# A fused spectral-mixing and gated-FFN kernel: the transfers of two small matrix sums move from the second run to the first, and some low parts, sums and silus change places

## The chip, the core and the metric

The kernel runs on one core of a Trainium2 chip. The metric is device time in microseconds (us), the median of several executions. The engines that appear below are PE (matrix multiply; its weight loads are listed as PEld), DVE (vector), ACT (activation), POOL and SP. SP and POOL also issue transfers (DMAs); each of them issues its own in program order.

## The reference

A layer norm of x (2048 tokens, 448 features) feeds two branches, whose product is added to x:

```python
xn = _layernorm(x, axis=-1)
a = jnp.einsum("bsd,ed->bse", xn, dft_hid_re)
b = jnp.einsum("bsd,ed->bse", xn, dft_hid_im)
s = jnp.einsum("ts,bse->bte", dft_seq_re, a) - jnp.einsum("ts,bse->bte", dft_seq_im, b)
g = _silu((_gelu(xn @ w_gate) * (xn @ w_up)) @ w_down)
return x + s * g
```

Everything is float32, the FFN has 1792 hidden columns, and x comes twice as the same array.

## The kernel before

Every float32 operand of a matmul is used as two parts: a high part, which ACT copies out in a rounded type, and a low part, which DVE makes as the value minus the high part. A product of two such operands takes three matmuls (high by high, high by low, low by high). The instruction order on each engine is written out by hand; nothing reorders it later.

**Stage 1, the FFN (up to about 403 us).** The 2048 tokens are four quarters of 512. Hidden columns come in blocks of 128, `f` = 0 to 13. After a start on the first two blocks, two runs follow: `p` = 0 (quarters 0 and 1) and `p` = 1 (quarters 2 and 3), each over `f` = 2 to 13, 24 blocks in all. A block is one call of `strassen`, which forms gate and up for both quarters with Strassen-like products `x1` to `x6`, and runs between them the down projections of an earlier pair of blocks (`down_one`, L439: tiles `po`, which DVE adds to `gacc` in L452). Between the products of a block three steps `prep` make the weights of the next block: ACT's plain high parts (L352), POOL's sums of weight parts (`sums_s`, L337 to L343), ACT's high parts of these sums (L356, L357), DVE's low parts (L353, L360, L361) and then SP's load of the weights after that (`load_s`, L319 and L320, into `raw`). `sums_s` also pops the list `adds`, behind its first sum: transfers that POOL issues with accumulation, among them those that form the sums of the sequence matrices in `sums` (L959). ACT's gelu of the first product is L526. In the first run and at the start of the second, `t_step` makes the operand sums of the second run: a DVE subtraction (L875), ACT's high part (L880) and DVE's low part (L884), from tiles that `t_load` brings into `tmp` (L860, L864).

Two buffers in DRAM, `e1[0]` and `e1[1]`, hold sums of the hidden-dimension DFT matrix `et`: `e_first` loads them (L1056, SP) and adds a second part with three POOL transfers (L1057, L1060). It is called in block `f` = 2 of the second run, and `e1` is read in the blocks `f` = 4 and 9 of that run. DVE's further sums of `et` (`e_sum`, L1064) end in `eq`, which SP stores in block `f` = 11 (`eq_store`, L1107).

**Stage 2, the hidden-dimension DFT (about 403 to 482 us).** Its order is the table `HID`: words such as `4.mm` (the matmuls of token tile 4), `4.ev` (ACT copies them out, L1386 and L1387), `4.sm` (four DVE sums, L1376 to L1379), `4.ca` and `4.lo` (high and low part, L1398 and L1401), `P3.le` (the low part of tile 15, L1345), `q.l` (three low parts of `eq`, L1087 and L1091), `s.3` and `s.all` (the last eight `po` tiles), `c.l4`, `c.s2`, `c.h2`, `c.d2` (load, sums, high part and low part of unit 4 or 2 of stage 3). A `c.d` issues a load into the place that it has read (`c.d0` unit 3, `c.d1` unit 6, `c.d2` unit 7).

**Stage 3, the sequence DFT (from about 482 us).** Eight pairs of row tiles `j`, each with 14 units `u` of Strassen-like products (L1534 high, L1537 low), then two plain tiles `t0`, `t1` (L1560). Per unit, `load_c` brings the matrices (L1439, L1440), `sum_c` adds (L1446, L1447), `high_c` and `low_c` split (L1454, L1458). The last pair gathers the products (`gather`, L1567 to L1575), takes silu of the FFN result (`gx`, loaded by L1514; L1639, L1693), multiplies and adds x, and stores.

Places that several of these share: unit 4 and 5 of stage 3 are loaded into the tile `f1`, which also holds tile 6 of stage 2 until `6.lo` has read it. In the lists of order below the names carry the program's own buffer numbers.

Of the kernel before, what the change touches and what calls it, by code (L numbers as in the profile page):

```python
# [10 lines left out]
AF = mybir.ActivationFunctionType  # L11
# [35 lines left out]
NS = len(KS)  # L47

LAST = 3


HID = """
0.mm l.0 q.h l.1 s.3 q.l 0.ev 0.sm 0.ca s.all 0.lo g.st 1.mm 1.ev 1.sm
P0.x1 P0.m 1.ca P0.x2 P0.u P0.x3 P0.c21 P0.x4 P0.be 1.lo P0.x1b P0.ac P0.x6 P0.bc P0.sc P0.cc
P0.x4b P0.ae P0.se 2.mm P0.ce P0.lc 2.ev P0.le 2.sm
P1.x1 P1.m 2.ca P1.x2 P1.u P1.x3 P1.c21 P1.x4 P1.be 2.lo P1.x1b P1.ac P1.x6 P1.bc P1.sc P1.cc
# [2 lines left out]
P2.x4b P2.ae  # L59
P3.x1 P3.m P2.ce P2.cc P3.x2 P3.u P3.x3 P3.c21 P2.le P3.x4 P3.be P3.x6 t.0 P2.lc P3.bc  # L60
P3.x1b P3.ac P3.sc P3.cc P3.x4b P3.ae c.l0
4.mm P3.ce P3.lc P3.le c.l1 c.l2 t.1 4.ev 4.sm 4.ca c.s0 c.s1
5.mm 4.lo 5.ev c.h0 5.sm c.d0 5.ca c.s2 6.mm 5.lo 6.ev 6.sm
7.mm c.h1 c.d1 c.h2 c.d2 6.ca c.s3 6.lo c.l4 c.l5 7.ev
"""


# [8 lines left out]
def fnet_geglu(ctx: ExitStack, tc: tile.TileContext, xw, ca, ct, cp, et, wss, wd, out):  # L76
# [495 lines left out]
    with tc.manual_schedule():  # L572
# [479 lines left out]
        e1 = [dram.tile([P, D], F32, name=f"e1{i}") for i in range(2)]  # L1052

        def e_first():
            for i in range(2):
                nc.sync.dma_start(e1[i], et[3 * i, :, 1])  # L1056
            adds.append(lambda: nc.gpsimd.dma_start(e1[0], et[1, :, 1], accum_op=ALU.add))  # L1057
            for r in (slice(0, 64), slice(64, P)):
                adds.append(
                    lambda r=r: nc.gpsimd.dma_start(e1[1][r], et[2, :64, 1], accum_op=ALU.add)  # L1060
                )

        def e_sum(to, a, b, n=P):
            return lambda: nc.vector.tensor_sub(*[e_part(i)[:n] for i in (to, a, b)])  # L1064
# [28 lines left out]
        def e_steps(f):  # L1093

            return {
                5: [e_sum(6, 0, 1), e_sum(5, 4, 0)],
                6: [e_sum(7, 2, 5), nop, es_high],
                7: [nop, es_low(0)],
                9: [nop, es_low(1), e_next],
                11: [e_sum(6, 2, 3), e_sum(7, 5, 2, n=64), then(e_sum(8, 0, 7), eq_store)],  # L1100
            }.get(f, [])

        def eq_at(i):
# [24 lines left out]
        for n, (p, f) in enumerate(blocks):  # L1128
            g = f // 2
            dn, q = [settle, send2] * 2, tq[p]  # L1130
            if n == len(blocks) - 2:
                v = sb.tile([P, 4096], FR, name="w2", tag="u0")
                slots.append((v[:, :WH], v[:, WH : WH + WL]))
                w2[0] = v
            prep = weights(n + 1)
            step = [e_steps(f)] if p else []
            if f % 2 == 0 and n:
                d_raw[0] = load_d(GROUPS[g])
            sum_step(n)
            if f % 2 and 1 < n < len(blocks) - 1 or n == len(blocks) - 2:  # L1140
                prep[1].append(lambda: weights_d(g))
                prep[2].append(lambda: low_of[g]())
            if p == 0:
                if f == 2:
                    dn = [nop, send, nop, send]
                    nc.sync.dma_start(gsp[0], gacc[2].rearrange("p k d -> p (k d)"))
                elif f == 3:
                    dn = [nop, send, send, low_d]
                if 6 <= f < 12:
                    step = [t1_steps[f - 6]]  # L1150
                elif f == 12:
                    step = [t1_steps[6][:1]]
                if f in (8, 11):

                    k = slice(0, 4, 3) if f == 8 else slice(1, 3)
                    for i in range(2):
                        v, w = [u[:, i * 2048 :][:, :2048] for u in (sp, a_x[1].bitcast(F32))]
                        v, w = [u.rearrange("p (k d) -> p k d", k=4)[:, k] for u in (v, w)]
                        nc.sync.dma_start(v, w)
            elif f == 2:  # L1160
                q = None
                for v, w in zip(prep, t1_steps[6][1:]):
                    v.append(w)
                dn[3] = then(send2, *t1_steps[7][:2])
                e_first()
            elif f == 3:

                late = then(late[0], t1_steps[7][2]), late[1]
                v = sb.tile([P, 8 * D], F32, name="gacc2", tag="u1")
                for c in range(2):  # L1170
                    gacc[2 + c] = part(v, c * 4 * D, 4, D)
                    nc.sync.dma_start(v[:, c * 4 * D :][:, : 4 * D], gsp[c])
            elif f == 4:
                e_begin()
            elif f == 5:
                nc.sync.dma_start(gs[:, : 8 * D], a_g[0])
            elif f == NF - 3:
                e_load(2)
            elif f == NF - 2:
                dn[2] = send2  # L1180
                prep[2].append(lambda: e_split(2))
                prep[2].extend([lambda b=b: e_load(b) for b in (1, 0, 3)])
            elif f == NF - 1:
                prep[1].append(lambda: e_split(0))
                prep[2].extend([lambda: e_split(3), lambda: e_split(1)])
                dn = [settle, send2, settle, nop]
                eq_load()
            while adds and n == len(blocks) - 1:
                adds.pop(0)()
            if step:  # L1190
                for v, w in zip(prep, step[0]):
                    v.append(w)
            prep = [then(*v) for v in prep]
            late = strassen(f, p, w_of[p, f], q, late, dn, prep)
            if p == 0 and f == 4:
                nc.sync.dma_start(gsp[1], gacc[3].rearrange("p k d -> p (k d)"))
            elif p == 0 and f == 5:
                t_load(0, 1, 0, 1)
            elif p == 0 and f == 9:
                t_load(0, 1, 3, 2)  # L1200
            if f % 2:
                dq += [(g, c, w_d[g], kk) for c in (2 * p, 2 * p + 1) for kk in range(4)]
# [313 lines left out]

        LOAD_AT = 2
        STORE_AT = 6, 9
        GX_AT, GX_END = (NS, 0), NS - LAST - 4

        PARTS = slice(0, 6, 5), slice(2, 4), slice(4, 7, 2), slice(1, 2)
        PRODUCTS = {1: (1, 0), 6: (3, 5), 2: (2, 2), 7: (5, 3), 5: (4, 4), 3: (6, 6), 4: (0, 1)}
# [73 lines left out]
        for m, (j, k) in enumerate(units):  # L1596
# [37 lines left out]
            if end and u == NS - LAST:  # L1634
# [1 line left out]
                prep_c(m + 4)  # L1636

                c12_6, c11_2, c21_7, c12_5, c22_5, c12_3, c21_4 = gather(ps)
                nc.scalar.activation(g_[0], gx[0], AF.Silu)  # L1639
                gather_1 = lambda: nc.vector.tensor_add(c1, c1, cs[1][1])  # L1640
                for f in (c12_6, c21_7, c12_5, c22_5, c21_4, gather_1, c11_2):
                    f()
# [5 lines left out]
            elif end and u > NS - LAST:  # L1648
                if u == NS:
                    py0 = py  # L1650
                if m < len(units) - 1:
                    continue
                y = raw_at(m + 3)[:, :D]
                nc.vector.tensor_add(c0, c0, py0[:, :D])
                nc.vector.tensor_mul(c0, c0, g_[0])
                nc.vector.tensor_add(c0, c0, x_[0])
                nc.sync.dma_start(ov[:, NK - 2], c0)
                halves_ = [
                    (e, eng, lambda p=p, e=e: nc.vector.tensor_mul(y[:, e], g_[1][:, e], p[:, e]))
                    for p, e, eng in zip(both_, sides, (nc.scalar, nc.sync))  # L1660
                ]
                for e, eng, times_ in halves_:
                    times_()
                    nc.vector.tensor_add(c1[:, e], c1[:, e], y[:, e])
                    eng.dma_start(ov[:, NK - 1, e], c1[:, e])
            elif u == NS - 1 and not end:
                todo = gather(ps)
                for f in todo[:3]:
                    f()
                prep_c(m + 3)  # L1670
            elif u == NS and not end:
                for f in todo[3:]:
                    f()
                prep_c(m + 3)
                nc.scalar.activation(kept, py[:, :D], AF.Copy)
            elif u == NS + 1:
                prep_c(m + 3)
                spare = [lambda: nc.vector.tensor_add(c0, c0, kept)]
                spare += give(j, 0)
                spare.append(lambda py=py: nc.vector.tensor_add(c1, c1, py[:, :D]))  # L1680
                spare += give(j, 1)
                banks = banks[1:] + banks[:1]
            else:
                if m:
                    prep_c(m + 3)
                if m == 4:
                    sums_of[7]()
                if m == 6:
                    hid_split(7)()
                if j and u in (1, 4):  # L1690
                    nc.scalar.activation(kept, gx[u // 4], AF.Silu)
                if end and u == NS - LAST - 1:
                    nc.scalar.activation(g_[1], gx[1], AF.Silu)  # L1693
                if spare:
                    spare.pop(0)()
                if (u in STORE_AT or end and u == STORE_AT[1] - 1) and stores:
                    stores.pop(0)()
# [66 lines left out]
```

## Time and profile before

| | |
|---|---|
| median of 3 runs | 774.96 us (774.65 to 775.76) |
| the profiled execution | 774.05 us |
| its span, first to last instruction | 772.3 us |
| mean granted PE clock | 0.998 |
| busy: PE, PEld, DVE, ACT, POOL | 98%, 89%, 85%, 46%, 16% of the span |
| DMA | 170.54 MB, mean 221 GB/s |

The profile is of one execution. Its page gives busy times and the costliest groups; the trace behind it gives every instruction with its start, its length, the idle time of its engine ahead of it and what released it. "x12" stands for twelve instructions of a kind in a row, and a row's length runs from the first one's start to the last one's end. Starts are in us from the span's start. In the list of waits the three numbers are total idle time in us, times, and the longest one.

### The profile page before, as it was taken

What the parts mean: (1) busy time and instruction counts of PE and PEld (TensorE: products, weight loads), DVE (VectorE), ACT (ScalarE), POOL (GpSimd) and SP (SyncE); (2) the same over time, 40 slices, a digit from 0 to 9 for tenths busy, and PEclk for the clock granted to TensorE, in tenths of its full rate; (3) what the DMA queues carried; (4) which work ended last, traced back from release to release, by engine and by line L of the source; (5) the groups of instructions that cost most, each with busy time, mean ns of one, the idle gap of its engine ahead of it and who ended that gap; (6) DMA issues with size and microseconds to landing.
All of it is one profiled execution on the core that took longest, in us unless ns stands there. A gap on an engine that the chain in (4) does not pass through costs nothing.

```text
span 772.3 us, 11563 instructions
## 1 busy us (share of the span) xinstructions
PE 759.8 (98%) x4033; PEld 683.5 (89%) x4033; DVE 654.2 (85%) x1120; ACT 355.4 (46%) x512; POOL 120.1 (16%) x163
## 2 busy tenths in 40 slices
PE   9999999999998899999999999999999999999997
PEld 8988888888886788888888999899999999999997
DVE  7987789899986888988986998788888797979787
ACT  6866443534432434433433446545444454544451
POOL 1002322313223423313400000000000000000000
PEclk9999999999999999999999999999999999999999
DMA  8077574949577592929652556779796979789793
GB/s 292 20 222 231 123 242 132 261 143 239 185 195 220 200 310 92 249 68 298 192 175 95 251 203 226 239 243 320 229 349 204 339 223 322 230 283 289 237 313 148
DMA packets 82923, 170.54 MB, mean 221 GB/s; under 512 B 8240, under 2 KB 63792, under 8 KB 80944
## 3 DMA queue, kind: packets, MB, share of 16 engines
q1 hardware_dynamic: 77232, 142.82, 53.5%
q0 software_dynamic: 5488, 26.87, 16.2%
q8 instruction: 31, 0.51, 0.3%
q14 instruction: 28, 0.23, 0.1%
q10 hardware_dynamic: 144, 0.11, 0.0%
HBM read 146.70 MB, written 53.08 MB: 259 GB/s over the span
## 4 chain that ended last, share of the span: by engine, by line
PE 83%; DVE 10%; DMA 3%; issue 2%; POOL 1%; ACT 1%; SPq 0%; DVEq 0%; POOLq 0%
PE p L1534 19%; PE x L465 18%; PE po L439 13%; PE p L1537 9%; PE ab L1278 5%; PE py L1560 4%; PE hx L1317 4%; PE x L477 3%; PE gu L388 3%; PE gu L621 2%; DMA e<-et 1%; DMA raw<-cp 1%; PE pt L223 1%; DVE gacc L452 1%; DMA out<-cc 1%
## 5 line engine op out<-in xcount | busy, mean ns | idle before, releaser
L439 PE MATMUL po<-wd,hs 128*128 128x448 f32 x672 | 146.3, 366 | 1.4 <-DVE gacc L452 1.4
L439 PEld LDWEIGHTS po<-wd,hs 128*128 128x128 f32 x672 | 125.7, 188 | 14.3 <-DVE gacc L452 2.2
L465 PE MATMUL x<-xt,w 128*128 128x512 f32 x432 | 113.3, 393 | 1.2 <-ACT tmp L526 1.2
L465 PEld LDWEIGHTS x<-xt,w 128*128 128x128 f32 x432 | 81.9, 190 | 17.8 <-ACT tmp L526 1.6
L465 PE MATMUL x<-t,w 128*128 128x512 f32 x276 | 80.5, 391 | 0.0
L1454 ACT ACTIVATE w<-raw 128x896 fp32r<-128x896 f32 (+1 forms) x58 | 52.7, 910 | 52.1 <-PE p L1534 20.9
L452 DVE TENSOR_TENSOR gacc<-gacc,po 128x448 f32<-128x448 f32 x96 | 58.6, 614 | 6.2 <-PE po L439 6.0
L542 ACT ACTIVATE hs<-tmp 128x512 fp32r<-128x512 f32 x24 | 15.2, 633 | 102.2 <-DVE tmp L540 102.2
L465 PEld LDWEIGHTS x<-t,w 128*128 128x128 f32 x276 | 51.7, 188 | 10.3 <-DVE tmp L544 0.4
L1586 POOL DMA_DIRECT2D cc<-xw x14 | 12.4, 883 | 291.8 <-DVE raw L1446 111.7
L1534 PE MATMUL p<-xt,xt 128*128 128x448 f32 x168 | 54.4, 374 | 0.0
L1534 PE MATMUL p<-ts_g,w 128*128 128x448 f32 x168 | 54.4, 374 | 0.0
L337 POOL TENSOR_TENSOR raw<-raw 128x256 f32<-128x256 f32 x23 | 18.8, 817 | 214.4 <-DMA raw<-wss 164.7
L1454 ACT ACTIVATE w<-f 128x896 fp32r<-128x896 f32 (+1 forms) x37 | 33.0, 892 | 41.5 <-PE p L1537 16.0
L1537 PE MATMUL p<-xt,xt 128*128 128x224 f32 x168 | 44.4, 264 | 0.0
L1537 PE MATMUL p<-ts_g,w 128*128 128x224 f32 x168 | 44.4, 264 | 0.0
L1458 DVE TENSOR_TENSOR w<-raw,w 128x896 fp32r<-128x896 f32 (+1 forms) x39 | 40.6, 1045 | 1.8 <-ACT w L1454 1.1
L356 ACT ACTIVATE w<-raw 128x768 fp32r<-128x768 f32 x24 | 20.3, 844 | 37.1 <-POOL raw L343 36.9
L1534 PE MATMUL p<-xt,w 128*128 128x448 f32 x112 | 36.4, 374 | 0.0
L1534 PE MATMUL p<-hs,w 128*128 128x448 f32 x112 | 35.6, 374 | 0.0
L477 PE MATMUL x<-xt,w 128*128 128x512 f32 x98 | 31.1, 397 | 3.5 <-ACT xt L880 2.7
L1278 PE MATMUL ab<-w,xt 128*128 128x448 f32 x128 | 33.7, 365 | 0.0
(306 smaller groups left out, 1869.1 us busy)
## 6 DMA issues: line engine op xcount, KB each, us to landing
sums<-ca SPq DMA_DIRECT2D x16, 896.0 KB, 8.8
sums<-ca POOLq DMA_DIRECT2D x16, 896.0 KB, 9.5
raw<-ct SPq DMA_DIRECT2D x69, 192.0 KB, 4.4
raw<-wss SPq DMA_DIRECT2D x24, 512.0 KB, 3.5
xt<-td SPq DMA_DIRECT2D x24, 448.0 KB, 5.5
ts_g<-td SPq DMA_DIRECT2D x24, 448.0 KB, 6.3
raw<-sums SPq DMA_DIRECT2D x69, 128.0 KB, 4.2
f<-ct SPq DMA_DIRECT2D x43, 192.0 KB, 3.6
```

Source lines behind the costliest of these rows:

```text
L388: nc.tensor.matmul(ps[:, cols], a, xt[:, k, cols], start=n == 0, stop=n == len(mm) - 1)
L439: nc.tensor.matmul(po[:, :D], hs[:, a, kk * P : (kk + 1) * P], wdn[:, b, i], start=n == 0, stop=n == 5,)
L452: nc.vector.tensor_add(ga, ga, po[:, :D])
L465: nc.tensor.matmul(ps, a[i], b[j], start=first and n == 0, stop=n == 2, skip_group_check=True)
L477: nc.tensor.matmul(ps, a[0], x_, start=False, stop=True, skip_group_check=True)
L1278: nc.tensor.matmul(ps[r], x_, e, start=start_, stop=stop_, skip_group_check=True)
L1317: nc.tensor.matmul(ps[i], a[:, sl], b, start=first and n == 0, stop=n == len(mm) - 1, skip_group_check=True,)
L1454: nc.scalar.activation(c_hl[m][0], raw_at(m)[:, :n], AF.Copy)
L1458: nc.vector.tensor_sub(l, raw_at(m)[:, : h.shape[-1]], h)
L1534: nc.tensor.matmul(ps[q][:, :D], h, v, start=u % UN == 0, stop=False, skip_group_check=True)
L1537: nc.tensor.matmul(ps[q][:, :HD], l, v[:, :HD], start=False, stop=u % UN == NS - 1, skip_group_check=True,)
L1560: nc.tensor.matmul(p[:, e], w, v[:, e], start=n == 0, stop=n == 11)
```

## The change

It reorders; no arithmetic is added or left out.

1. The two loads of `e1` go to block `f` = 7 of the first run, its three accumulating transfers into `adds` in block `f` = 9 of the first run.
2. In the second run the sum `e_sum(6, 2, 3)` goes from block 11 to block 10, and the other two of block 11 one step ahead, with the store of `eq`.
3. In `HID`, `q.l` goes from ahead of `0.ev` to behind `g.st`; `P3.le` behind `4.ca`; `c.s1`, `c.s2`, `c.d0`, `c.d1`, `c.d2`, `c.s3` and `c.h2` to other places around `5.ca`, `6.ca` and `6.lo`.
4. At the end the loads of `gx` come one unit later, and its two silus stand together behind the copy of the first product.

```diff
 HID = """
-0.mm l.0 q.h l.1 s.3 q.l 0.ev 0.sm 0.ca s.all 0.lo g.st 1.mm 1.ev 1.sm
+0.mm l.0 q.h l.1 s.3 0.ev 0.sm 0.ca s.all 0.lo g.st q.l 1.mm 1.ev 1.sm
...
         def e_first():
-            for i in range(2):
-                nc.sync.dma_start(e1[i], et[3 * i, :, 1])
             adds.append(lambda: nc.gpsimd.dma_start(e1[0], et[1, :, 1], accum_op=ALU.add))
...
-                11: [e_sum(6, 2, 3), e_sum(7, 5, 2, n=64), then(e_sum(8, 0, 7), eq_store)],
+                10: [nop, e_sum(6, 2, 3)],
+                11: [e_sum(7, 5, 2, n=64), then(e_sum(8, 0, 7), eq_store)],
...
             if p == 0:
...
+                if f == 7:
+                    for i in range(2):
+                        nc.sync.dma_start(e1[i], et[3 * i, :, 1])
+                elif f == 9:
+                    e_first()
...
             elif f == 2:
                 q = None
...
-                e_first()
...
-        GX_AT, GX_END = (NS, 0), NS - LAST - 4
+        GX_AT, GX_END = (NS, 0), NS - LAST - 3
...
                 c12_6, c11_2, c21_7, c12_5, c22_5, c12_3, c21_4 = gather(ps)
-                nc.scalar.activation(g_[0], gx[0], AF.Silu)
+                for v, w in ((g_[1], gx[1]), (g_[0], gx[0])):
+                    nc.scalar.activation(v, w, AF.Silu)
...
-                if end and u == NS - LAST - 1:
-                    nc.scalar.activation(g_[1], gx[1], AF.Silu)
```

**POOL around the sums of `e1`.** Each group L337 to L343 is one block's `sums_s`. Before, these are its rows in the first block of the second run (`e_813` and `e_814` are `e1[0]` and `e1[1]`):

```order
L337 TENSOR_TENSOR raw<-raw 128x2x128
L1057 DMA e_813<-et 128x448
L1060 DMA e_814<-et 64x448 x2
L340 TENSOR_TENSOR raw<-raw 128x2x128
L341 TENSOR_TENSOR raw<-raw 128x128
L342 TENSOR_TENSOR raw<-raw 64x128
L343 TENSOR_TENSOR raw<-raw 128x256
```

On the same engine in the changed kernel, the block `f` = 9 of the first run:

```order
L337 TENSOR_TENSOR raw<-raw 128x2x128
L1055 DMA e_813<-et 128x448
L1058 DMA e_814<-et 64x448 x2
L340 TENSOR_TENSOR raw<-raw 128x2x128
L341 TENSOR_TENSOR raw<-raw 128x128
L342 TENSOR_TENSOR raw<-raw 64x128
L343 TENSOR_TENSOR raw<-raw 128x256
```

The three transfers have left the second run, where L340 now follows L337 directly, and stand in the same way in a block five blocks earlier. On SP the two loads that they add to have gone from just behind the two `sums` transfers of the second run's first block to a place seven blocks earlier.

**DVE at the start of stage 2**, before: the last sum of `s.3`, then the low parts of `q.l` (L1087, L1091), the four sums of tile 0 (L1376 to L1379) and the first sums of `s.all`.

```order
L452 TENSOR_TENSOR gacc_2207<-gacc_2207,po_2_2_3448 128x448
L1087 TENSOR_TENSOR w<-w 128x896
L1091 TENSOR_TENSOR w_3185<-raw,w_3185 64x448
L1091 TENSOR_TENSOR w<-raw,w 64x448
L1376 TENSOR_TENSOR raw<-raw 128x224
L1377 TENSOR_TENSOR raw<-raw 128x224
L1378 TENSOR_TENSOR raw<-raw 128x224
L1379 TENSOR_TENSOR raw<-raw 128x224
L452 TENSOR_TENSOR gacc_2207<-gacc_2207,po_2_3_3466 128x448
```

DVE in the changed kernel from the same row on:

```order
L452 TENSOR_TENSOR gacc_2207<-gacc_2207,po_2_2_3448 128x448
L1379 TENSOR_TENSOR raw<-raw 128x224
L1380 TENSOR_TENSOR raw<-raw 128x224
L1381 TENSOR_TENSOR raw<-raw 128x224
L1382 TENSOR_TENSOR raw<-raw 128x224
L452 TENSOR_TENSOR gacc_2207<-gacc_2207,po_2_3_3463 128x448
L452 TENSOR_TENSOR gacc_2207<-gacc_2207,po_3_0_3471 128x448
L452 TENSOR_TENSOR gacc_2207<-gacc_2207,po_3_1_3479 128x448
L452 TENSOR_TENSOR gacc_2207<-gacc_2207,po_3_2_3487 128x448
L452 TENSOR_TENSOR gacc_2207<-gacc_2207,po_3_3_3495 128x448
L1404 TENSOR_TENSOR w_3185<-raw,w_3185 128x7x224
L1085 TENSOR_TENSOR w<-w 128x896
```

The three low parts of `q.l` (of which the last row shows the first, now L1085) have moved from ahead of five sums of `po` tiles to behind them and behind the low part of tile 0.

**DVE at the end of stage 2**, before: the sums of tile 6 (on `f_3539`, which is `f1`), the low parts of units 1 and 2 of stage 3 (L1458 x2), the sums of unit 3, the low part of tile 6 (L1401, the last reader of tile 6 in `f1`).

```order
L1376 TENSOR_TENSOR f_3539<-f_3539 128x224
L1377 TENSOR_TENSOR f_3539<-f_3539 128x224
L1378 TENSOR_TENSOR f_3539<-f_3539 128x224
L1379 TENSOR_TENSOR f_3539<-f_3539 128x224
L1458 TENSOR_TENSOR w<-raw,w 128x896 x2
L1446 TENSOR_TENSOR raw<-raw 128x128
L1447 TENSOR_TENSOR raw<-raw 128x128
L1401 TENSOR_TENSOR ts_g_4002<-f_3539,ts_g_4002 128x7x224
```

The same place in the changed kernel:

```order
L1379 TENSOR_TENSOR f_3539<-f_3539 128x224
L1380 TENSOR_TENSOR f_3539<-f_3539 128x224
L1381 TENSOR_TENSOR f_3539<-f_3539 128x224
L1382 TENSOR_TENSOR f_3539<-f_3539 128x224
L1461 TENSOR_TENSOR w<-raw,w 128x896
L1449 TENSOR_TENSOR raw<-raw 128x128
L1450 TENSOR_TENSOR raw<-raw 128x128
L1404 TENSOR_TENSOR ts_g_3993<-f_3539,ts_g_3993 128x7x224
L1461 TENSOR_TENSOR w<-raw,w 128x896
L1449 TENSOR_TENSOR raw<-raw 128x128
L1450 TENSOR_TENSOR raw<-raw 128x128
```

The low part of tile 6 (now L1404) stands ahead of the low part of unit 2 and of the sums of unit 3. PE's own order is the same in both kernels.

6 lines of the change are left out of this document (3 added, 3 removed).

## The prediction

> **What bounds the kernel now.** I read the page's busy times first, then the list of waits, then PE's timeline around each wait.
>
> ```profile
> PE 759.8 (98%) x4033; PEld 683.5 (89%) x4033; DVE 654.2 (85%) x1120; ACT 355.4 (46%) x512; POOL 120.1 (16%) x163
> ```
>
> ```profile
> PE x L477 <- ACT xt L880: 2.7, 1, 2.7
> PE po L439 <- DVE gacc L452: 1.4, 2, 1.2
> PE x L465 <- ACT tmp L526: 1.2, 1, 1.2
> PE p L1537 <- DVE xt L1458: 0.9, 1, 0.9
> PE x L477 <- DVE xt L884: 0.8, 1, 0.8
> ```
>
> PE is busy for 98% of the span, so a reordering can only win what PE waits, and what lies behind PE's last matmul. The list names six waits of 7.0 us in all; three are neighbours. What they really cost is read from PE's pace around them:
>
> ```profile
> 239.82 1.52 PE L465 MATMUL x<-xt,w 128*128 128x512 f32 x6
> 241.18 0.61 PE L477 MATMUL x<-xt,w 128*128 128x512 f32 x2
> 241.63 2.59 PE L439 MATMUL po<-wd,hs 128*128 128x448 f32 x12
> ...
> 257.87 2.59 PE L439 MATMUL po<-wd,hs 128*128 128x448 f32 x12
> ...
> 407.72 7.46 PE L439 MATMUL po<-wd,hs 128*128 128x448 f32 x36
> 416.42 2.70 PE L439 MATMUL po<-wd,hs 128*128 128x448 f32 x12 [1.25 <-DVE gacc L452]
> ```
>
> ```profile
> 245.40:257.80 12.40, 8.89 (x27) 0.86 0.55 201
> 255.00:260.00 5.00, 5.00 (x19) 0.72 0.07 26
> ```
>
> (The second fence shows windows: stretch, its length, PE's busy time and matmuls, granted clock, DMA share, GB/s.) Unhindered, six 512-wide matmuls take 241.18 - 239.82 = 1.36 us, 0.227 each; 448-wide ones (7.46 - 2.59) / 24 = 0.203. Twelve of these from 241.63 and the 27 of the window would end at 241.63 + 12 x 0.203 + 27 x 0.227 = 250.2; the next row starts at 257.87. **This place costs 7.7 us**, not the listed 4.7: behind the waits the granted clock falls to 0.72, and matmuls run at about half pace for a while.
>
> Why PE waits there:
>
> ```profile
> 229.05 1.24 SPq L1056 DMA_DIRECT2D e<-et  x2
> ```
>
> ```profile
> 231.84 0.80 POOL L337 TENSOR_TENSOR raw<-raw 128x256 f32<-128x256 f32 x1 [9.89 <-DMA raw<-wss]
> 238.82 0.81 POOL L1057 DMA_DIRECT2D e<-et  x1 [6.18 <-DMA e<-et]
> ...
> 240.41 1.64 POOL L340 TENSOR_TENSOR raw<-raw 128x256 f32<-128x256 f32 x1
> ```
>
> ```profile
> 243.72 0.84 ACT L356 ACTIVATE w<-raw 128x768 fp32r<-128x768 f32 x1 [9.65 <-POOL raw L343]
> ```
>
> ```profile
> 244.60 0.96 DVE L360 TENSOR_TENSOR w<-raw,w 128x768 fp32r<-128x768 f32 x1 [7.01 <-ACT w L356]
> ...
> 250.57 0.80 DVE L875 TENSOR_TENSOR tmp<-tmp 128x512 f32<-128x512 f32 x1
> 251.29 1.21 DVE L562 TENSOR_TENSOR tmp<-tmp 128x512 f32<-128x512 f32 x1
> ```
>
> The loads of `e1` are issued at 229.05 and land some 9 us later; POOL stands on them for 6.18 us in the middle of the weight sums, then spends 1.6 us (238.82 to 240.41) issuing three transfers. The sums end just before 243.72; ACT's high parts wait there, and with them the gelu behind them on ACT (PE's first wait); DVE's low part idles 7.01 us, and the operand step L875, L880, L884, on which PE's other two waits hang, follows it.
>
> **The change part by part.** *Loads and accumulations of `e1` in the first run.* Both reasons for POOL's stop go. L340 follows L337 at about 232.6; the four sums need 243.7 - 240.4 = 3.3 us, so ACT gets them at 236 and is through with L356 and L357 by 237.2. DVE reached L360 at 244.60 - 7.01 = 237.6, so it does not wait. L875 comes 7 us earlier, at 243.6, and ACT's high part is ready at 245.0 (0.63 each for what ACT has to do). PE, 12 matmuls from 241.63 and then 14 of the next block, wants it at 244.07 + 14 x 0.227 = 247.2: two us to spare. No wait is left, and with no idle there is nothing to slow the clock. **Minus 7.7 us**; the bounds are -7.7 and, if the operand step's two waits with the slow clock behind them stayed (2.7 + 0.8 + 8 matmuls x 0.2), -2.6. I take -7.7, since each link has its margin.
>
> What it adds: in block `f` = 9 of the first run POOL issues three transfers, 1.6 us by the rows above, and SP two. The loads go out two blocks ahead, some 25 us; they took 9. POOL's end moves by about 2 us, and ACT's high parts with it:
>
> ```profile
> 164.93 0.85 ACT L356 ACTIVATE w<-raw 128x768 fp32r<-128x768 f32 x1
> ...
> 174.12 0.64 ACT L542 ACTIVATE hs<-tmp 128x512 fp32r<-128x512 f32 x1 [5.66 <-DVE tmp L540]
> ```
>
> ACT has 5.66 us of idle later in that block; the block behind it, which has two such transfers already, shows no wait of PE. Cost nothing; without that cover, 2 us.
>
> A row that tells against it: DVE's L562 takes 1.21 us at 251.29, where one of its kind takes 0.68, beside POOL's sums. Without the stop POOL's sums run from 232.6 to 236 beside a busy DVE, which may stretch DVE by 0.5 us a row, one or two rows; the margin of 2 us holds that. The Trainium skill ("SBUF — State Buffer", Who interferes with whom) says that a vector instruction with two SBUF inputs and a GpSimd one that reads SBUF exclude each other, the later one blocked until the other ends; by that rule a DVE row would lose up to one POOL row, and the trace agrees in size, 0.5 us here.
>
> *`q.l` behind the sums of `s.all`.*
>
> ```profile
> 412.10 1.08 DVE L1087 TENSOR_TENSOR w<-w 128x896 fp32r<-128x896 f32 x1
> ...
> 414.41 0.39 DVE L1376 TENSOR_TENSOR raw<-raw 128x224 f32<-128x224 f32 x1
> ...
> 415.75 0.61 DVE L452 TENSOR_TENSOR gacc<-gacc,po 128x448 f32<-128x448 f32 x1
> ```
>
> The low parts hold DVE from 412.10 to 414.41, so the next `po` tile is drained at 415.75 and PE, which needs its place, starts at 416.42 where 36 x 0.203 from 407.72 gives 415.03. Without them DVE drains it 2.3 us earlier. PE gains 1.39 plus 0.11 (2.70 against 2.59), **1.5 us**. The low parts then run where DVE would wait for the copies of tile 1; their first user, `P0.x2`, comes a whole tile later (22 matmuls, 4.5 us).
>
> *`P3.le`, `6.lo`, `c.d2`.*
>
> ```profile
> 490.56 0.38 PE L1534 MATMUL p<-ts_tmp,xt 128*128 128x448 f32 x1
> 491.87 0.37 PE L1537 MATMUL p<-ts_tmp,xt 128*128 128x224 f32 x1 [0.93 <-DVE xt L1458]
> ```
>
> ```profile
> 483.50 1.78 DVE L1401 TENSOR_TENSOR ts_g<-f,ts_g 128x1568 fp32r<-128x1568 f32 x1
> ...
> 488.40 0.29 DVE L1446 TENSOR_TENSOR f<-f 128x128 f32<-128x128 f32 x1 [2.12 <-DMA f<-sums]
> ```
>
> ```profile
> 485.31 0.33 SPq L1439 DMA_DIRECT2D f<-ct  x1
> ```
>
> Unit 4's load waits for tile 6's last reader (483.50 + 1.78 = 485.3), its sums for the load (488.40), PE for its low part. The chain of tiles 4, 5, 6 on DVE loses `P3.le` (about 1.0), and `6.lo` a low part and two sums (1.6), less what stands ahead of it now: I place it at 481.7, 1.8 us earlier, and the low part as much. The wait of 0.93 goes, with 0.1 that it adds to the matmul behind it: **1.0 us**; bounds 0 and 1.2. Unit 7's load now comes 1.4 us later; it is wanted three units later.
>
> *The sums and the store of `eq`.*
>
> ```profile
> 387.72 1.54 PE L465 MATMUL x<-xt,w 128*128 128x512 f32 x6
> 389.41 2.70 PE L439 MATMUL po<-wd,hs 128*128 128x448 f32 x12 [0.15 <-DVE gacc L452]
> ```
>
> ```profile
> eq<-ew SPq DMA_DIRECT2D x1, 896.0 KB, 5.0
> ```
>
> ```profile
> 376.15 1.10 POOL L337 TENSOR_TENSOR raw<-raw 128x256 f32<-128x256 f32 x1 [6.54 <-DMA raw<-wss]
> ```
>
> ```profile
> 381.06 0.40 ACT L357 ACTIVATE w<-raw 128x256 fp32r<-128x256 f32 x1
> ```
>
> ```profile
> 383.71 0.95 DVE L360 TENSOR_TENSOR w<-raw,w 128x768 fp32r<-128x768 f32 x1
> ```
>
> PE's start at 389.41 should be 387.72 + 6 x 0.227 = 389.08: 0.33, and 0.11 on the row, 0.4 us. DVE is behind there without a break, so one sum of 0.6 less in block 11 wins it: **0.4 us**. In exchange the 896 KB store now stands on SP ahead of the weights for which POOL waits at 376.15. It goes out some 1.5 us before them, so they land up to 1 us later (0 to 5, the store's whole time); DVE's low part at 383.71 has its input from ACT at 381.46, so 2.2 us are free. Cost nothing.
>
> The Trainium skill ("DMA: Bandwidth & Descriptors", Queues, rings and completion order) speaks against this: a ring's descriptors are consumed in order, so the weights would stand behind the whole store. No run here shows it; what it would give is the third rival.
>
> *The silus.* PE's last matmul is not the end: DVE's last 17 rows run, from
>
> ```profile
> 759.94 0.62 DVE L1571 TENSOR_TENSOR cc<-cc,p 128x448 f32<-128x448 f32 x1 [0.47 <-DMA out<-cc]
> ```
>
> without a break. That row waits for a store, not for ACT. ACT is earlier by a silu, DVE is not: nothing, with -0.5 and +0.5 as bounds.
>
> The sum: 7.7 + 1.5 + 1.0 + 0.4 = 10.6. The profiled execution took 774.05 (span 772.3 and 1.75 around it), so 763.4; the median of the runs, 774.96, lies 0.91 above it, and I carry that: **764.3 us**.
>
> **The rivals.**
> - *Only the large place goes* (chance 0.20). The three small waits return a little later, because DVE's work is the same and only its order is not. For it: DVE is at 85%. Against: DVE has idle behind each of the three. 774.96 - 7.7 = 767.3, or between this and 764.3.
> - *The operand step stays late* (0.05): its transfers into `tmp` or DVE's order, not POOL, set the two waits. Against: L875 has no idle ahead of it. 764.3 + 5.1 = 769.4.
> - *The weights stand behind the store* (0.05), 5.0 us late: less the 2.2 free, 2.8 are lost, 767.1. By the Trainium skill's rule on rings, above, this is what comes.
> - *The change doesn't do what it says* (0.02): POOL stops on the loads in the first run as long as it did in the second, with the same follow-up. 764.3 + 7.7 = 772.0, and the small waits too make it 774.96, no change.
> - *Slower* (0.02): the same store of `eq`, if SP first waits for DVE's last sum and the weights land much later. Up to 2.2 us late costs nothing, each us beyond it one us of PE; the point from which the kernel is slower than before is 2.2 + 10.6 = 12.8 us late; at 15 it takes 777.2. Against: the sum stands ahead of the low part for which the weights' load waits anyway.
>
> **How the numbers follow.** The forecast, 764.3, has 0.66. The range: down to 763.4 (the tail's 0.5, the 0.2 more at the small wait, and the runs' spread), up to 767.4, which takes in the first and third rival: 0.91. A measurement of this kernel can tell about 0.2% from no change. Faster 0.96 (forecast, first three rivals), same 0.02, slower 0.02.
>
> **What would show it.** In the new trace: no wait of PE on L880, L884 or L526 between 240 and 258 and a granted clock of 1.00 there; POOL's L340 directly behind L337 in the second run's first block; the accumulations around 162 with no wait of PE in the two blocks behind; 48 `po` matmuls without a gap around 408 to 417 (now 9 us earlier); no wait on unit 4's low part; the last DVE rows unchanged. It is wrong if PE waits anew for ACT or DVE in the block of the transfers or in the last block of stage 1, or if the second run's first block still shows a wait.

## The result, and the profile after

The changed kernel takes **763.76 us** (median of 4 runs, 763.10 to 764.47), the kernel before 774.96 beside it (median of 3, 774.65 to 775.76; a fourth run, disturbed, is left out). The ratio is 0.9854, 95% interval 0.9834 to 0.9873: 1.5% less time, well clear of no change. The forecast was 764.3, with a range of 763.4 to 767.4. The profiled execution took 764.14 (span 762.4), so it is 9.9 us shorter than the profiled one of before.

The page's busy times, and PE's list of waits, all of it, of the changed kernel:

```profile
PE 756.3 (99%) x4033; PEld 682.4 (90%) x4033; DVE 656.3 (86%) x1120; ACT 355.5 (47%) x512; POOL 123.1 (16%) x163
```

```profile
PE warm L590 <- PEq L1756: 0.8, 1, 0.8
PE pt L705 <- issue: 0.5, 1, 0.5
PE gu L605 <- ACT xt L723: 0.3, 1, 0.3
```

None of the six waits of before is left; these three belong to the start. PE's busy time fell too, by 3.5 us; 2.7 of these are at the large place, where matmuls ran at a slow clock or started anew after a wait. The window of the changed kernel with the matmuls that ran from 247.3 to 257.9 before (its columns: the stretch, its length, busy time and instructions of PE, PEld, DVE, ACT and POOL, granted clock, DMA share, GB/s):

```profile
246.00:251.00 5.00, 4.92 (x22) 3.72 (x22) 5.00 (x8) 4.36 (x7) 3.12 (x4) 1.00 0.60 241
```

The clock is 1.00; before, it was 0.86 over 245.4 to 257.8. The rows around the large place (start, duration, engine, line, operands, idle time and what ended it):

```profile
234.14 0.90 POOL L337 TENSOR_TENSOR raw<-raw 128x256 f32<-128x256 f32 x1 [9.58 <-DMA raw<-wss]
235.01 1.32 POOL L340 TENSOR_TENSOR raw<-raw 128x256 f32<-128x256 f32 x1
...
238.35 0.85 ACT L356 ACTIVATE w<-raw 128x768 fp32r<-128x768 f32 x1 [3.23 <-POOL raw L343]
...
239.23 0.96 DVE L360 TENSOR_TENSOR w<-raw,w 128x768 fp32r<-128x768 f32 x1 [0.98 <-ACT w L356]
...
245.20 0.85 DVE L875 TENSOR_TENSOR tmp<-tmp 128x512 f32<-128x512 f32 x1
245.46 1.19 POOL L340 TENSOR_TENSOR raw<-raw 128x256 f32<-128x256 f32 x1
245.97 1.22 DVE L562 TENSOR_TENSOR tmp<-tmp 128x512 f32<-128x512 f32 x1
...
247.12 0.94 DVE L884 TENSOR_TENSOR xt<-tmp,xt 128x512 fp32r<-128x512 f32 x1
...
247.65 0.97 PE L477 MATMUL x<-xt,w 128*128 128x512 f32 x2
```

POOL's L340 follows L337 without a stop, ACT waits 3.2 instead of 9.7, DVE 1.0 instead of 7.0. But L337 started at 234.1 where the forecast used 231.8, L875 at 245.2 where it used 243.6, and the two matmuls L477 take 0.97 instead of 0.61: the second one had to wait a little for L884. The margin of 2 us was used up.

PE issues the same 4033 matmuls in every kernel here, in the same order. So the time from one given matmul to another can be compared between profiles, and the excess over the shortest is what a place cost. The table has it for the four places of the prediction (named by their time in the changed kernel), and the stretch behind PE's last matmul; the rows below the first two are the experiments, one profiled execution each; the column of times has the medians of all their runs. The kernel before had 774.36, 774.48 and 774.74 us on the three chips of the experiments.

```
kernel            us (runs)    247    382    408    482   tail
before            774.96 (3)  7.69   0.30   1.51   1.20   4.29
changed           763.76 (4)  0.38   0.01   0.00   0.00   4.28
e1_back           772.78 (8)  7.73   0.03   0.00   0.00   4.24
e1_alone          765.62 (4)  0.00   0.03   1.51   1.28   3.74
e1_loads_early    763.08 (4)  0.00   0.03   0.00   0.00   3.71
e1_loads_ahead    765.72 (4)  1.80   0.03   0.00   0.00   3.89
ql_back           765.83 (4)  0.94   0.03   1.51   0.00   3.71
tiles_back        764.60 (4)  0.00   0.00   0.00   1.19   4.27
eq_back           763.66 (4)  0.23   0.75   0.00   0.00   3.71
silu_back         763.58 (4)  0.81   0.01   0.00   0.00   4.32
after_again       763.52 (4)  1.03   0.09   0.00   0.00   3.72
no_sums_14        763.05 (4)  0.00   0.07   0.00   0.00   3.87
adds_behind       766.79 (6)  4.99   2.21   0.00   0.00   4.03
early_behind      765.47 (4)  0.88   0.47   0.00   0.00   4.26
```

Before to changed: 7.31 + 0.29 + 1.51 + 1.20 = 10.3 us, less 0.4 that this execution lost in its first 190 us and another one of the same kernel (after_again) did not, gives the 9.9 of the spans.

### The profile page after: what moved, and what is told of

Read it like the earlier page. It is cut to its first block, busy times and chain, and to the rows that moved or that the text cites. A ratio compares the mean times of both kernels' runs of the same rounds, so it can differ in the third digit from the quotient of the medians.

```text
span 762.4 us, 11568 instructions
## 1 busy us (share of the span) xinstructions
PE 756.3 (99%) x4033; PEld 682.4 (90%) x4033; DVE 656.3 (86%) x1120; ACT 355.5 (47%) x512; POOL 123.1 (16%) x163
## 4 chain that ended last, share of the span: by engine, by line
PE 84%; DVE 8%; DMA 4%; issue 2%; POOL 1%; ACT 1%; SPq 0%; DVEq 0%; POOLq 0%
PE p L1537 20%; PE x L465 18%; PE po L439 14%; PE p L1540 9%; PE ab L1281 5%; PE py L1563 4%; PE hx L1320 4%; PE gu L388 3%; PE x L477 3%; PE gu L621 2%; DMA raw<-wss 1%; DMA raw<-cp 1%; PE pt L223 1%; DMA out<-cc 1%; DMA raw<-xw 1%
## 5 line engine op out<-in xcount | busy, mean ns | idle before, releaser
L465 PE MATMUL x<-xt,w 128*128 128x512 f32 x432 | 112.1, 390 | 0.0
L337 POOL TENSOR_TENSOR raw<-raw 128x256 f32<-128x256 f32 x23 | 19.1, 830 | 211.2 <-DMA raw<-wss 179.2
L1537 PEld LDWEIGHTS p<-ts_g,w 128*128 128x128 f32 x168 | 31.5, 187 | 2.4
```

Of the source, the lines that this page charges most:

```text
L465: nc.tensor.matmul(ps, a[i], b[j], start=first and n == 0, stop=n == 2, skip_group_check=True)
L1537: nc.tensor.matmul(ps[q][:, :D], h, v, start=u % UN == 0, stop=False, skip_group_check=True)
```

## The experiments

**The large place.** Four kernels ask what made it. *e1_back* undoes the e1 edit alone:

```diff
-                if f == 7:
-                    for i in range(2):
-                        nc.sync.dma_start(e1[i], et[3 * i, :, 1])
-                elif f == 9:
-                    e_first()
...
                 dn[3] = then(send2, *t1_steps[7][:2])
+                for i in range(2):
+                    nc.sync.dma_start(e1[i], et[3 * i, :, 1])
+                e_first()
```

> The changed kernel with the loads and accumulations of e1 back in the second run's first block; all else as changed. Theory (POOL's stop on the landing of these loads made the three waits and the slow clock behind them): the wait of PE on the gelu and the two on the operand step are back between 240 and 258 us, PE's pace falls there again, and PE's last matmul ends 7.3 us later (771.4 us; the forecast's term is 7.7). Rival (part of the gain is not of this edit, but of how the four edits work together): 2 to 5 us later, 766 to 769 us.

770.97 us in the profiled execution, the lowest of its eight runs (up to 773.11); ratio to before 0.9977 (0.9967 to 0.9987). PE's waits, and the window behind them:

```profile
PE x L477 <- ACT xt L880: 2.6, 1, 2.6
PE x L465 <- ACT tmp L526: 1.3, 1, 1.3
PE x L477 <- DVE xt L884: 0.8, 1, 0.8
```

```profile
252.00:257.00 5.00, 4.11 (x11) 3.03 (x12) 4.90 (x8) 3.96 (x7) 2.40 (x3) 0.73 0.51 206
```

The three waits and the slow clock are back, at 7.73 us, and nothing else is. The theory holds for the profiled execution. By the medians the edit is worth more, 772.78 - 763.76 = 9.0 us, and the section on the rivals comes back to that. The other half is *e1_alone*, the kernel before with this edit only.

> The kernel before with the e1 edit alone. Theory: 7.3 to 7.7 us under the kernel before (about 767 us), and PE's waits at 389, 416 and 492 us, 7 us earlier, stay as long as they were (0.15, 1.25, 0.93 us). Rival (the edits are not independent: once the large place is gone, DVE is elsewhere at the small ones): a small wait grows or goes, and the gain is off 7.3 by over 0.5 us.

765.62 us, ratio 0.9889 (0.9872 to 0.9905): 8.7 under before by the medians, where 7.3 to 7.7 was expected. In the profiles it is 8.3: the whole 7.69 at the large place, and most of the rest in the tail, 0.55. The waits at 408 and 482 are about as long as before:

```profile
PE po L439 <- DVE gacc L452: 1.2, 1, 1.2
PE p L1539 <- DVE xt L1460: 1.0, 1, 1.0
```

But the small one at 382 is gone, without the edit that was made for it. The expectation was wrong there; eq_back takes that up.

*e1_loads_early* puts only the accumulations back, into the block where they stood (the loads stay at `f` = 7):

```diff
-                elif f == 9:
-                    e_first()
...
                 dn[3] = then(send2, *t1_steps[7][:2])
+                e_first()
```

> The changed kernel with the loads of e1 early, but its three accumulations issued again by POOL in the second run's first block. It tells the wait for the landing (6.2 us) from the issuing (1.6 us). Theory now (with the accumulations in block f = 9 POOL and DVE fall behind by over a us and stay so to the second run's first block; without them POOL starts its sums there up to 1.9 us earlier, and the issuing eats 1.6): the time of the changed kernel within 0.4 us, 763.7 to 764.5 us. Rival (the prediction's margin of 2 us was there, and issuing costs on top of it): 0 as well, but with POOL's first sum at the same time as in the changed kernel, 234 us, and ACT's high part 1.6 us later than there. Second rival (issuing in this block is itself a large part of the 7.3): 1.5 us or more slower.

763.08 us (762.76 to 764.13), 0.6 under the expected range, but not to be told from the changed kernel. POOL's rows, and DVE's at the operand step:

```profile
231.51 0.99 POOL L337 TENSOR_TENSOR raw<-raw 128x256 f32<-128x256 f32 x1 [9.71 <-DMA raw<-wss]
232.44 0.81 POOL L1055 DMA_DIRECT2D e<-et  x1
232.99 1.93 POOL L1058 DMA_DIRECT2D e<-et  x2
234.04 1.66 POOL L340 TENSOR_TENSOR raw<-raw 128x256 f32<-128x256 f32 x1
...
244.67 0.68 DVE L875 TENSOR_TENSOR tmp<-tmp 128x512 f32<-128x512 f32 x1
245.27 0.68 DVE L562 TENSOR_TENSOR tmp<-tmp 128x512 f32<-128x512 f32 x1
...
246.05 1.05 DVE L884 TENSOR_TENSOR xt<-tmp,xt 128x512 fp32r<-128x512 f32 x1
```

So the issuing alone costs PE nothing in this block: without the wait for the landing none of the 7.7 us is lost. (No run has the wait without the issuing.) And POOL starts its sums here at 231.5 instead of 234.1, 2.2 us earlier against PE's matmuls, as the theory says. But in e1_alone and tiles_back, with the accumulations in block `f` = 9 like the changed kernel, POOL starts at 232.3 and 231.9 in the changed kernel's time, against 232.0 here. So not the accumulations alone made the changed kernel late.

*e1_loads_ahead* asks why the loads took 9 us to land. They and the accumulations are back in the second run's first block, but the loads stand on SP ahead of the two copies of `sums`:

```diff
+            if p and f == 2:
+                for i in range(2):
+                    nc.sync.dma_start(e1[i], et[3 * i, :, 1])
             sum_step(n)
```

> The changed kernel with loads and accumulations of e1 again in the second run's first block, but the two loads issued on SP ahead of the two copies of sums instead of behind them. Theory (the loads landed 9 us after their issue because they stood behind 1.8 MB on the same queue): they land at about 234.5 us, POOL's stop is 1.5 to 2 us instead of 6.2, and the kernel is 1 to 1.5 us slower than the changed one (about 765 us). Rival (a copy from DRAM to DRAM takes its 8 to 9 us whatever stands ahead of it): they land near 237, POOL stops for 4 to 5 us, and the kernel is 5 us or more slower (769 us).

765.72 us, ratio 0.9886 (0.9871 to 0.9901). How long the loads took from issue to landing, in e1_back and here (each view of the issues: KB each, us to landing), and POOL's stop here:

```profile
e<-et SPq DMA_DIRECT2D x2, 224.0 KB, 9.2
```

```profile
e<-et SPq DMA_DIRECT2D x2, 224.0 KB, 5.7
```

```profile
233.90 0.81 POOL L1055 DMA_DIRECT2D e<-et  x1 [1.54 <-DMA e<-et]
```

The stop is 1.5 instead of 6.2, PE loses 1.8, a little more than the 1 to 1.5 expected: the loads were late because of the copies ahead of them in the queue, not by themselves.

**The small places.** Each edit undone alone in the changed kernel: *ql_back* puts `q.l` back into its old place in the list, *tiles_back* the list's last three rows, *eq_back* the sum and the store.

```diff
-                10: [nop, e_sum(6, 2, 3)],
-                11: [e_sum(7, 5, 2, n=64), then(e_sum(8, 0, 7), eq_store)],
+                11: [e_sum(6, 2, 3), e_sum(7, 5, 2, n=64), then(e_sum(8, 0, 7), eq_store)],
```

> The changed kernel with q.l back ahead of tile 0's drain. Theory (the low parts hold DVE for 2.3 us while PE needs a place of po): PE waits again on DVE's gacc about 36 matmuls after 400.5 us, for 1.2 us, and everything behind it is 1.5 us later (about 765.2 us). Rival (DVE has the same work, and PE waits a little later instead, so that the wait was only moved): under 0.5 us later at the end.

> The changed kernel with the old order of P3.le, 6.lo, c.d2 and their neighbours in the last rows of the list. Theory (unit 4's load waits for tile 6's last reader, its sums for the load, PE for the low part): PE waits about 0.9 us on unit 4's low part near 482, and the end is 1.0 to 1.2 us later (about 764.9 us). Rival (the load would be late by itself, so that DVE's order does not set it): 0.3 us or less.

> The changed kernel with the sum of e and the store of eq back in block f = 11 as before. Forecast as the prediction had it (one DVE row less in that block wins the time at 389): PE is 0.3 to 0.4 us later from about 382 on. Theory now (the kernel with the e1 edit alone, in which this sum was not moved, won the same 0.28 us at that place): no shift there, 0.1 us or less, and the weights that POOL waits for near 369 land no earlier than in the changed kernel by more than 1 us. Time 763.4 to 764.5 us either way.

Of ql_back's list of waits, of tiles_back's timeline of PE, and of eq_back's:

```profile
PE po L439 <- DVE gacc L452: 1.2, 1, 1.2
```

```profile
480.98 0.38 PE L1537 MATMUL p<-ts_tmp,xt 128*128 128x448 f32 x1
482.27 0.37 PE L1540 MATMUL p<-ts_tmp,xt 128*128 128x224 f32 x1 [0.91 <-DVE xt L1461]
```

```profile
380.21 1.54 PE L465 MATMUL x<-xt,w 128*128 128x512 f32 x6
...
382.36 2.70 PE L439 MATMUL po<-wd,hs 128*128 128x448 f32 x12 [0.62 <-DVE gacc L452]
```

`q.l` is worth 1.51 us and the tiles' order 1.19, each at its place, as the theories said (ql_back's 0.94 at 247 lies within the scatter found below). eq_back went against the theory: 0.75 us come back, more than the forecast's 0.4. Without this edit the place cost 0.30 (before), 0.03 (e1_alone) and 0.75; with it 0.00 to 0.09 in nine of eleven profiles, and more only in the two in which all accumulations stand behind the sums. DVE runs there without a break, so whether it is late may depend on where it stood some blocks ahead; that is not shown. By the medians eq_back is no slower (763.66). What the store does to the weights behind it (changed, then eq_back):

```profile
raw<-wss SPq DMA_DIRECT2D x1, 512.0 KB, 4.0
```

```profile
raw<-wss SPq DMA_DIRECT2D x1, 512.0 KB, 3.5
```

They take 0.5 us longer, no more, and nothing waits for them.

*silu_back* undoes the silus' move.

> The changed kernel with the silus as before. Theory (DVE's last 17 rows wait for a store and not for ACT): PE's shift is 0 everywhere, and the stretch behind PE's last matmul is one of the two that the profiles so far show, 3.7 to 3.9 us or 4.2 to 4.3 us, set by when the store of cc has landed. Rival (the silu on ACT ahead of the copy holds DVE's first row of the tail): that stretch is 4.6 us or more.

763.58 us, and a tail of 4.32, the upper of two levels. These come from a store, as the same row shows in the changed kernel and, one line number lower and with the row behind it, in e1_loads_early:

```profile
750.02 0.62 DVE L1574 TENSOR_TENSOR cc<-cc,p 128x448 f32<-128x448 f32 x1 [0.86 <-DMA out<-cc]
```

```profile
748.44 0.62 DVE L1573 TENSOR_TENSOR cc<-cc,p 128x448 f32<-128x448 f32 x1
749.35 0.62 DVE L1574 TENSOR_TENSOR cc<-cc,p 128x448 f32<-128x448 f32 x1 [0.28 <-PE p L1539]
```

Where the store has landed in time, this row doesn't wait, the next one waits for PE alone, and the last rows end 0.5 us sooner. Both levels are found with either order of the silus (3.74 and 4.29 with the old one), so the move is worth nothing that shows.

**The rest at the large place.** The 0.4 us there varied from kernel to kernel without a reason in their edits. Four more runs: the changed kernel again; without POOL's weight sums in the block behind; with the accumulations behind the sums; and that with e1_loads_early.

> The changed kernel once more, unaltered. In the profiles so far with the e1 edit as it is, PE lost 0, 0, 0.2, 0.4, 0.8 and 0.9 us at the place near 247 us, though the instructions up to there are the same in all but the waits' history. Theory (this rest is scatter from one execution to the next, set by where POOL's sums of the following weights fall beside DVE's operand step): another value between 0 and 0.9 us there, and 0 at the other three places; 763.0 to 764.5 us. Rival (each kernel has its own rest): 0.4 us again.

763.52 us, ratio 0.9850 (0.9835 to 0.9864), and 1.03 us at the large place: a little over what was expected, and far from the 0.38 of the first profile. It is scatter, in one and the same kernel.

```profile
244.82 0.74 POOL L337 TENSOR_TENSOR raw<-raw 128x256 f32<-128x256 f32 x1 [7.67 <-DMA raw<-wss]
244.96 1.14 DVE L875 TENSOR_TENSOR tmp<-tmp 128x512 f32<-128x512 f32 x1
245.51 1.19 POOL L340 TENSOR_TENSOR raw<-raw 128x256 f32<-128x256 f32 x1
246.03 1.22 DVE L562 TENSOR_TENSOR tmp<-tmp 128x512 f32<-128x512 f32 x1
...
247.17 0.94 DVE L884 TENSOR_TENSOR xt<-tmp,xt 128x512 fp32r<-128x512 f32 x1
...
248.17 0.50 PE L477 MATMUL x<-xt,w 128*128 128x512 f32 x1 [0.73 <-DVE xt L884]
```

DVE's three rows stand beside POOL's and take 1.14, 1.22 and 0.94 us. *no_sums_14* leaves POOL's five sums of this block out:

```diff
+            def sums():
+                if n == 14:
+                    while adds:
+                        adds.pop(0)()
+                else:
+                    sums_s(nc.gpsimd)
...
-            return [plain, lambda: sums_s(nc.gpsimd)], [high], [low, *next_]
+            return [plain, sums], [high], [low, *next_]
```

> The changed kernel without POOL's five weight sums in the second block of the second run (those that start near 245 us); it leaves these sums out, so that block's weights are wrong. Theory (DVE's rows L875, L562 and L884 take up to 1.2 us instead of 0.68 because POOL's sums run beside them, and that makes the last of them late for PE): all three take 0.68 to 0.70 us and PE loses 0.1 us or less at the place near 247 us. Rival (DVE is late there because of what stands ahead of it, and would be without POOL too): the three rows may be short, but PE loses 0.4 to 0.9 us as in four of six profiles.

763.05 us, and nothing lost at the place:

```profile
244.33 0.68 DVE L875 TENSOR_TENSOR tmp<-tmp 128x512 f32<-128x512 f32 x1
...
244.93 0.69 DVE L562 TENSOR_TENSOR tmp<-tmp 128x512 f32<-128x512 f32 x1
...
245.71 0.69 DVE L884 TENSOR_TENSOR xt<-tmp,xt 128x512 fp32r<-128x512 f32 x1
```

From the start of L875 to the end of L884 it is 2.07 us, against 3.15 in after_again; the difference, 1.1, is what PE lost there. DVE did start 0.6 us earlier here too. The short rows alone would have done: in after_again PE could have taken the part 0.227 us behind the matmul that starts at 247.05, at 247.28, and 244.96 + 2.07 is 247.0. The earlier start alone would not quite: 244.33 + 3.15 is 247.5. The Trainium skill ("SBUF — State Buffer", Who interferes with whom) says that a vector instruction with two SBUF inputs and a GpSimd one that reads SBUF block each other; these rows agree.

*adds_behind* moves the loop over `adds` in `sums_s` behind the last of the five sums; *early_behind* does it in e1_loads_early.

```diff
-        while adds:
-            adds.pop(0)()
         eng.tensor_sub(r[:, 3:15:11], r[:, 7:13:5], r[:, 0:14:13])
...
         eng.tensor_sub(r[:, 4:6], r[:, 8:11:2], r[:, 2:7:4])
+        while adds:
+            adds.pop(0)()
```

> The changed kernel with POOL's accumulating transfers, those of e1 and of sums, issued behind the five weight sums of a block instead of behind the first of them. Theory (what costs in block f = 9 is not the transfers but that their 1.6 us of issuing hold up the sums): ACT gets POOL's last sum there 1.6 us earlier than in the changed kernel, DVE's low part in the blocks behind is 0.8 us or more earlier against PE, and PE loses 0.1 us or less near 247 us; 763.0 to 763.8 us. Rival (the weights land later because the accumulations share the DMA engines): POOL's first sum in the second run's first block stays as late as in the changed kernel, and so does DVE.

> Loads of e1 early, its accumulations in the second run's first block, and all accumulations behind the sums: the version that should leave no wait at all. Theory: POOL's last sum in that block ends 1.6 us earlier than with the accumulations in the middle (235.4 instead of 237.8), PE loses 0.1 us or less near 247 us; 762.7 to 763.6 us, which is 0.1% under the changed kernel at best and may not be told from it. Rival (sums that end earlier start the next weights' load and sums earlier, so that these fall beside DVE's operand step): PE loses 0.3 us or more near 247 us.

Both were meant to gain and lost: 766.79 us (765.41 to 770.22; the profiled execution is the slowest) and 765.47 (764.83 to 767.41). In block `f` = 9 the theory is right: POOL's last sum ends at 166.8 instead of 168.7, 1.5 of this against PE's matmuls. The loss comes five blocks later (adds_behind; POOL and SP, then the issues between 224.0 and 227.2):

```profile
222.46 1.67 POOL L959 DMA_DIRECT2D sums<-ca  x2
...
225.86 0.33 SPq L319 DMA_DIRECT2D raw<-wss  x1
...
236.92 1.37 POOL L337 TENSOR_TENSOR raw<-raw 128x256 f32<-128x256 f32 x1 [12.79 <-DMA raw<-wss]
```

```profile
raw<-wss SPq DMA_DIRECT2D x1, 512.0 KB, 10.0
```

The accumulations of `sums` (1.8 MB) went out 2.5 us later, at 222.5 instead of 219.9, and the weights that SP issued behind them needed 10.0 us instead of 6.5 in the changed kernel (5.1 before). In eleven of the fourteen profiles the weights of this block land 1.2 us behind the second accumulation (1.19 to 1.25), whenever either was issued; in the changed kernel's first 0.8 behind it, and in the two here, where the accumulations went out last, 0.3 behind it and 0.6 ahead. Counted from the first accumulation's issue, the weights land 13.2 to 13.9 us later in all fourteen, whether SP issues them 3.4 or 8.8 us behind it. So what delays POOL in one block delays the weights of the next, and with them POOL again. By this path a lag of POOL reaches the second run's first block with PE showing nothing between. The rival's words (POOL stays as late) were too mild: POOL came 2.8 us later still. In early_behind the accumulations go out at 220.8, POOL starts at 235.2, and DVE's row L875 so late that PE loses 0.9 us though the rows are short:

```profile
246.10 0.69 DVE L875 TENSOR_TENSOR tmp<-tmp 128x512 f32<-128x512 f32 x1
246.70 0.68 DVE L562 TENSOR_TENSOR tmp<-tmp 128x512 f32<-128x512 f32 x1
```

So the rest has two causes, a late start and shared rows; early_behind loses by the first with short rows, after_again by both.

## Why the prediction was right, step by step

**The bound and the mechanism** were right: PE's waits went, no engine took their place, and the places at 247, 408 and 482 answer each to its own edit. (The clock of 0.72 behind the waits is a mean over 5 us; in the trace it is 0.50 for 3.41 us, shown at the end.)

**Loads and accumulations of e1, forecast 7.7:** 7.3 in the first profile, 6.7 in the second, 7.7 in two others with the same edit (e1_alone, tiles_back). The mechanism is shown from both sides, and e1_loads_early adds that without the wait for the landing nothing is lost. The step that was off is "two us to spare". Three things ate it. The weights landed later than at 231.7, since in both profiles of the changed kernel a lag of POOL came along from the first run; "cost nothing" for the accumulations in block `f` = 9 was right for PE in the next blocks, but such a lag reaches five blocks on. How much of it is theirs stays open, since e1_alone and tiles_back have them and no lag there. Port sharing was looked for beside the sums of the same block (232.6 to 236), where it costs nothing; it falls on the operand step, beside the sums of the block behind. And the margin was worked out for ACT's high part only; the low part, L884, comes last. So the sign "no wait of PE on L880, L884 or L526" held in the first profile, and not in after_again, where PE waits 0.73 us on L884.

**`q.l`, forecast 1.5:** 1.51, both ways.

**`P3.le`, `6.lo`, `c.d2`, forecast 1.0:** 1.20, both ways, at the upper bound. The term was mis-sized in the reading: the listed wait of 0.93 counts from the modelled end of the matmul ahead, but unhindered the next one starts 0.17 before that end (0.38 long, 0.21 from start to start). 0.93 + 0.17 + 0.1 is 1.20. The mechanism came as worked out: tile 6's low part starts at 472.9, which is 481.6 in the time of before, and the forecast placed it at 481.7.

**The sum and store of `eq`, forecast 0.4:** 0.3 in the first pair, 0.75 undone alone, 0 in e1_alone. These are single executions, and by the medians nothing shows, so that the edit gains anything is not shown. The weights behind the store cost nothing, as forecast: they landed 1.2 us behind the store, 0.5 later than without it.

**The silus, forecast 0:** nothing that shows, inside the bounds of 0.5.

**From the sum to the time.** 10.6 was forecast between the profiled executions, 9.9 came. The addition of 0.91 for the median did not carry over: the changed kernel's median lies 0.4 below its profiled execution. The two misses partly cancel: 763.4 + 0.9 forecast, 764.1 - 0.4 measured. That the time came within 0.6 us is in part luck.

**The rivals.** None came. "Only the large place goes" is refuted at 408 and 482. "The weights stand behind the store" has the order right and the price wrong. Of the rest, whether the medians' larger gain (11.2 us here and with after_again) is more than scatter of the kernel before stays in part open: e1_back's runs lie up to 2.1 us above its profiled one. The clocks on record point at a reason. In before's runs beside the experiments and in e1_back's, 37 in all, the mean granted clock was 0.998 in 10, e1_back's profiled one among them, and 0.993 to 0.996 in 27; before's profiled execution had 0.998 too. In the other kernels' runs it was 0.998 to 1.000. So in most executions the large place, or another, cost more of the clock than in those profiled; no trace shows where.

No version tried is measurably faster than the changed kernel. What is left at the large place is what its two profiles lost there, 0.4 and 1.0 us; in e1_loads_early, and in no_sums_14, which leaves work out, it is nothing.

## What to carry to other kernels

A place with a wait is priced by the time between two given matmuls on both sides, not by the listed wait: the slow clock behind it and the overlap of matmuls are in the first, not in the second. An engine that stands on a transfer in the middle of work others need is the first thing to look for, and the transfer's place in its queue the second. A margin worked out on one part's chain holds only if it is worked out for the part that comes last, with the rows as they run beside the other engines, and with transfers still under way from the blocks before.

## What the runs showed of the hardware

- Transfers of two queues hold each other up: weights on SP's queue landed 1.2 us behind POOL's accumulation in eleven profiles, and over all fourteen took 4.5 to 10.0 us for the same 512 KB. The Trainium skill ("DMA: Bandwidth & Descriptors", Queues, rings and completion order) says that the write to a transfer's semaphore lands only after every earlier write of that DMA engine, across its queues; that could give such a landing, but no run here tells it from shared bandwidth, and in adds_behind the weights landed 0.6 us ahead of the accumulation.
- In the fourteen profiles the granted clock is recorded in steps of 3.41 us: it changes only at whole multiples of 3.41 us from the record's start. PE's busy share of a step went with the clock of the next one. Behind all 17 steps with a share of 0.45 or less, most of them at the kernels' ends, the next step had half the clock; behind all others, the lowest at 0.48, it had the full one. At the large place of before (1.42 of 3.41 us busy), and at a wait of adds_behind near 390 us (1.84 of 3.41), each step with the one behind it:

```profile
250.93:254.34 3.41, 1.42 (x5) 0.97 (x6) 3.41 (x5) 2.59 (x4) 3.33 (x4) 1.00 0.90 353
254.34:257.75 3.41, 3.41 (x10) 2.66 (x9) 3.25 (x5) 1.99 (x3) 0.15 (x1) 0.50 0.14 57
```

```profile
387.01:390.42 3.41, 1.84 (x9) 1.73 (x10) 3.38 (x7) 0.76 (x2) 0.00 (x0) 1.00 1.06 221
390.42:393.83 3.41, 3.41 (x17) 2.89 (x16) 1.50 (x3) 1.62 (x3) 0.00 (x0) 1.00 0.95 348
```

So a wait of 1.1 us (e1_loads_ahead) or 0.7 (after_again) at the large place cost no clock, while 2.2 and 0.8 in a row (adds_behind, 0.78 of 3.41 us busy) cost one step at half clock. If this holds in general, the same waits cost a step or none, by how they fall into the steps (no run here tries that).

- DVE's 128x512 rows took 0.68 us alone and up to 1.23 beside POOL.
